# The first six row blocks of a weight, loaded in nine transfers instead of one, at the end of a decode kernel

## The chip, the cores and the metric

The kernel runs on one core of one Trainium2 chip. The metric is the device time of one execution in microseconds (us): the median of several runs.

## The reference, cut to what matters

One decode step mixes an attention block (a) and a small feed-forward block (b) by a gate that is computed from the input.

```python
x = A_x                                             # (2, 1, 512)
g = _sigmoid((x * gate_w).sum(-1, keepdims=True))
a = _A_ref(x, A_k_cache, A_v_cache, A_wq, A_wo)     # 2 x 32 heads, 4096 cached keys of 128, then @ wo
b = _B_ref(x, B_w1, B_w2)                           # relu(x @ w1) @ w2, inner size 1376
return g * a + (1 - g) * b
```

Keys and values are 64 MB each in bf16, wq and wo 4 MB each, w1 and w2 1.4 MB each. Nearly all that the kernel does in time is to bring 145 MB through the DMA engines.

## The kernel before, in words

All loads are issued by SyncE (SP) on one queue, in the order in which the program lists them, and the core's 16 DMA engines work that queue off. The order is w1, wq, ten key transfers, nine value transfers (`jobs` 0 to 8, each of 4 or 8 MB), wo in two pieces (`wo0` of 3 MB, `wo1` of 1 MB), and w2. Each transfer names a semaphore; each DMA engine that takes part adds 1 to it when its share has landed, and the reader waits for 16. Transfers that must not overwrite data still in use have a wait of SP ahead of them. w2 reuses the memory of the transposed keys and of the probabilities (the tile `kt`), so its first transfer waits until the last probabilities have been copied out (`pt_8_0` to `pt_8_3`). The later w2 transfers have no wait of their own.

The pieces of w2, of 128 partitions each, and their semaphores are, in order of issue (sizes for one partition):

- `w2a`: row block 10 (1 KB).
- `w2b`: row blocks 0 to 5 (6144 bytes, 768 KB in all). This is the transfer that is changed.
- `w2c`: row blocks 6 and 7 and the first half of 8 (2560 bytes).
- `w2d`, `w2e`, `w2f`: the first half of row block 9, the second half of 8, the second half of 9 (512 bytes, 64 KB in all, each).

In the sources these rows are contiguous: partition p holds rows 10p to 10p+9 of w2 (`w2_in`), 10 KB in a row, of which `w2b` takes the first 6 KB.

TensorE's order at the end is fixed by hand. It multiplies the last value unit (`v_unit(8)`, L461), gathers the heads (`o_gather`, L486 and L496), projects with wo (`project`, L508, which waits for `wo0` at its row 0 and `wo1` at its row 24), and then sums the feed-forward part into the bank `fin`: row block 10 (`ffn_f(10)`, waits for `w2a`), the projected attention (`wo_sum`, L540), row blocks 0 to 7 (`ffn_f(0)` to `ffn_f(7)`, L516, of which row block 0 waits for `w2b` and row block 6 for `w2c`), and row blocks 8 and 9 in `ffn_last` (L208), which waits for `w2d`, `w2e` and `w2f` in that order. VectorE and ScalarE copy the four quarters of the result out (L579, L581), and SP and ScalarE send one row of it each (L293).

The lines of the transfers are L282 (values), L283 and L284 (wo), L285 (`w2a`) and L290 (`w2b` to `w2f`). L600 is the end of the program, where each engine's list is written out.

## Time and profile before

| what | us |
|---|---|
| median of 3 runs | 344.19 (344.06 to 344.74) |
| profiled execution, first to last instruction (span) | 342.9 |
| median less span: what lies around the span | 1.3 |
| TensorE busy / VectorE busy in the span | 197.8 / 178.5 |
| DMA moved in the span | 145.46 MB read, mean 425 GB/s |
| share of the span in which the chain that ended last stood on DMA | 68% |

The profiled execution has no time of its own beside its span; the sums below are made on the span and set on the median, with the 1.3 us that lie around it taken as unchanged. Besides the page, the trace holds a record of each DMA packet (start, duration, size, queue) and of each semaphore increment; where the text speaks of one DMA engine, packets were joined to a chain, each at the end of the one before it, which works because the engines are never idle between 6 us and the end.

### The profile page before, as it was taken

The numbers are of one execution on the slowest core, as the hardware profiler recorded it, in microseconds if no ns is written. First come the engines' busy times: TensorE is split into PE (matmuls) and PEld (weight loads), VectorE is DVE, ScalarE is ACT, GpSimd is POOL, SyncE is SP. The second block draws the span as 40 slices with busy tenths as digits, with TensorE's granted clock in tenths as the row PEclk, the third lists the DMA queues.
The fourth block names the chain that finished last, engine by engine and source line by source line (L and its number), as shares of the span: only waits on it lengthen the run. The fifth ranks groups of instructions, "written<-read, shape, count | busy, mean of one in ns | idle before, by whom it ended". The sixth has DMA issues, their size and how long they took to land.

```text
span 342.9 us, 2540 instructions
## 1 busy us (share of the span) xinstructions
PE 197.8 (58%) x1228; PEld 54.3 (16%) x972; DVE 178.5 (52%) x127; ACT 23.1 (7%) x71; POOL 19.9 (6%) x36
## 2 busy tenths in 40 slices
PE   0177329799969799699799337220706043150656
PEld 0141001111111111111111013100303011020231
DVE  2239059899789899698999562220100103020121
ACT  1040000000000000000000240000000000000000
POOL 8000000000000000000000040110100101000000
PEclk9999959989999999989999858755656756565787
DMA  8998989899998999999999999999999999998996
GB/s 348 428 489 369 482 375 482 382 474 413 438 489 367 429 443 466 392 459 390 475 420 436 461 390 420 445 466 413 443 413 445 428 428 443 413 468 382 440 401 239
DMA packets 4196, 145.61 MB, mean 425 GB/s; under 512 B 469, under 2 KB 986, under 8 KB 1242
## 3 DMA queue, kind: packets, MB, share of 16 engines
q1 hardware_dynamic: 4178, 145.46, 98.5%
q8 instruction: 8, 0.13, 0.2%
q14 instruction: 2, 0.02, 0.0%
q10 hardware_dynamic: 8, 0.00, 0.0%
HBM read 145.46 MB, written 0.00 MB: 424 GB/s over the span
## 4 chain that ended last, share of the span: by engine, by line
DMA 68%; DVE 15%; PE 13%; ACT 1%; issue 1%; POOL 0%; SPq 0%; DVEq 0%
DMA kv<-in_A_k_cache_dram 31%; DMA kv<-in_A_v_cache_dram 23%; DVE kt L386 13%; DMA kt<-in_B_w_dram 9%; PE PS L461 6%; DMA kv<-in_A_wq_dram 4%; PE PS L407 3%; PE PS L197 3%; ACT kt L428 1%; PE PS L333 1%; DVE mpad L413 1%; DVE kt L471 1%; POOL ptm L444 0%; DVE qbuf L467 0%; DVE kt L432 0%
## 5 line engine op out<-in xcount | busy, mean ns | idle before, releaser
L386 DVE STREAM_TRANSPOSE kt<-kv 128x2048 f32<-128x2048 f32 x64 | 141.2, 2274 | 22.4 <-DMA kv<-in_A_k_cache_dram 22.3
L407 PE MATMUL PS<-kt,qbuf 128*128 128x512 bf16 x256 | 105.7, 413 | 31.8 <-DVE kt L386 26.3
L197 PE MATMUL PS<-kt,qbuf 128*128 128x512 bf16 x256 | 105.1, 411 | 0.0
L461 PE MATMUL PS<-kv,ptm 128*32 128x512 bf16 x512 | 46.5, 541 | 79.0 <-DMA kv<-in_A_v_cache_dram 76.0
L467 DVE TENSOR_TENSOR qbuf<-PS,maskc 128x512 f32<-128x512 f32 x9 | 6.2, 692 | 109.0 <-PE PS L461 109.0
L407 PEld LDWEIGHTS PS<-kt,qbuf 128*128 128x128 bf16 x256 | 25.5, 100 | 139.9 <-DVE kt L386 72.7
L461 PEld LDWEIGHTS PS<-kv,ptm 128*32 128x32 bf16 x512 | 19.0, 129 | 105.1 <-issue 98.6
L444 POOL COPY ptm<-kt 32x512 bf16<-32x512 bf16 (+1 forms) x18 | 11.5, 638 | 268.7 <-DVE rsum L475 175.6
L360 ACT ACTIVATE qbuf<-PS 32x8 bf16<-32x8 bf16 x40 | 7.9, 196 | 134.2 <-PE PS L197 132.7
L448 ACT ACTIVATE ptm<-kt 32x512 bf16<-32x512 bf16 (+1 forms) x9 | 5.3, 603 | 100.1 <-PE PS L461 98.7
L471 DVE TENSOR_REDUCE kt<-qbuf 128x128 f32<-128x512 f32 x9 | 9.3, 1028 | 0.3
L428 ACT ACTIVATE kt<-PS,negm 128x512 bf16<-128x512 f32 x8 | 5.4, 696 | 30.4 <-DVE negm L424 30.4
L333 PE MATMUL PS<-kv,xTw 128*32 128x512 bf16 x32 | 3.6, 629 | 5.9 <-DMA kv<-in_A_wq_dram 5.9
L478 PE MATMUL PS<-rsum,sell 128*32 128x1 f32 x4 | 0.4, 196 | 10.1 <-DVE rsum L475 10.1
L432 DVE STREAM_TRANSPOSE kt<-kt 128x1024 bf16<-128x1024 bf16 x4 | 5.0, 1245 | 1.7 <-ACT kt L428 1.4
L348 DVE CAST qrow<-PS 128x256 bf16<-128x256 f32 x2 | 2.4, 1396 | 6.4 <-PE PS L333 6.4
L508 PE MATMUL PS<-kv,oW 128*2 128x512 bf16 x32 | 3.4, 590 | 1.4 <-DMA kv<-in_A_wo_dram 1.4
L300 PE MATMUL PS<-ident,x_sb 3*128 3x3 bf16 x4 | 0.3, 166 | 6.2 <-DMA x_sb<-in_gate_w_dram 6.2
L486 PE MATMUL PS<-kt,selx 128*32 128x128 f32 x18 | 3.4, 328 | 0.3 <-DVE kt L471 0.3
L303 DVE COPY xT<-PS 128x12 bf16<-128x12 bf16 x1 | 0.2, 169 | 6.5 <-PE PS L300 6.5
L230 POOL MEMSET ptm<- 128x4096 bf16 x1 | 3.5, 3501 | 0.0
L413 DVE TENSOR_REDUCE mpad<-PS 128x1 f32<-128x2048 f32 x1 | 2.3, 2290 | 2.1 <-PE PS L197 2.1
(64 smaller groups left out, 44.2 us busy)
## 6 DMA issues: line engine op xcount, KB each, us to landing
kv<-in_A_k_cache_dram SPq DMA_DIRECT2D x4, 4096.0 KB, 31.6
kv<-in_A_v_cache_dram SPq DMA_DIRECT2D x2, 4096.0 KB, 27.0
kv<-in_A_wq_dram SPq DMA_DIRECT2D x1, 4096.0 KB, 15.0
kv<-in_A_wo_dram SPq DMA_DIRECT2D x1, 3072.0 KB, 29.3
kt<-in_B_w_dram SPq DMA_DIRECT2D x1, 1376.0 KB, 5.8
kv<-in_A_wo_dram SPq DMA_DIRECT2D x1, 1024.0 KB, 31.3
kt<-in_B_w_dram SPq DMA_DIRECT2D x1, 768.0 KB, 31.9
kt<-in_B_w_dram SPq DMA_DIRECT2D x1, 320.0 KB, 32.3
```

The source lines that it names most:

```text
L197: return e.add_instruction(mybir.InstMatmult(start_tensor_calc=start, stop_tensor_calc=stop, tile_size=(128, 128), tile_position=(0, 0), l ...
L333: pe(lambda e, n=n, t=t: e.matmul(psf(32 * (n % 4), 32 * (n % 4) + 32, (QR_B + n // 4) * BANK, 512), lhsT=xTw[:, t, :], rhs=wq_sb[:, t, n ...
L360: act(lambda a, hq=hq: a.activation(out=qbuf[32 * hq:32 * hq + 32, g % 2, :, :, 32 + 32 * hq], in_=cols[32 * hq:32 * hq + 32, u4 // 2, 2 * ...
L386: dve(lambda v: v.transpose(out=dst, in_=pairs[:, h, 64 * rr:64 * rr + 64]), waits=([f"pe_sc_{i - NKT}"] if i >= NKT else ["pe_h"] if i == ...
L407: return e.matmul(args[0], lhsT=args[1], rhs=args[2], start=first, stop=last)
L413: dve(lambda v: v.tensor_reduce(out=mpad[:, 0:1], in_=psf(0, 128, 0, 2048), axis=AX.X, op=ALU.max), waits=["pe_sc_63", "c_mpad"], signal=" ...
L428: act(lambda a, bk=bk, e2=e2: a.activation(out=blocks[:, bk, :, 16 * e2:16 * e2 + 16], in_=psf(0, 128, bk * BANK, 512).rearrange("p (r n) ...
L444: pool(lambda e, args=args: e.tensor_copy(**args), waits=waits, signal=f"pt_{j}_{hq}")
L448: act(lambda e, args=args: e.activation(func=ACT.Copy, **args), waits=waits, signal=f"pt_{j}_{hq}")
L461: pe(lambda e, m=m, t=t: e.matmul(psf(32 * t, 32 * t + 32, V_B[j % 2] * BANK, 512), lhsT=ptm[:, j % 2, 4 * m:4 * m + 4, :, :], rhs=rows[:, ...
L467: dve(lambda e: e.tensor_tensor(out=Y.rearrange("p (c d) -> p c d", c=4), in0=psf(0, 128, V_B[u % 2] * BANK, 512).rearrange("p (c d) -> p ...
L471: dve(lambda e: e.tensor_reduce(out=X2[:, u, :], in_=Y.rearrange("p (c d) -> p d c", c=4), axis=AX.X, op=ALU.add), waits=[f"dve_y{u}"], si ...
```

## The change

The rows of `w2b` are no longer fetched by one transfer of 128 partitions but by nine, which together cover the same partitions, with the same bytes for each. The first has 64 partitions (every second), the next 32 (every fourth from 1), the next 16 (every eighth from 3). The sixteen partitions left (7, 15, ..., 127) come in transfers of 5, 4, 3, 2, 1 and 1 rows. All nine add to the same semaphore, so TensorE now waits for 144 at row block 0 in place of 16. `w2a` stays ahead of them and `w2c` to `w2f` behind them in SP's list.

```diff
+    parts = [slice(0, 128, 2), slice(1, 128, 4), slice(3, 128, 8)]
+    parts += [slice(a, b + 1, 8) for a, b in ((7, 39), (47, 71), (79, 95), (103, 111), (119, 119), (127, 127))]
     for name, c0, c1 in (("w2b", 0, 3072), ("w2c", 3072, 4352), ("w2d", 4608, 4864), ("w2e", 4352, 4608), ("w2f", 4864, 5120)):
-        sp(lambda e, name=name, c0=c0, c1=c1: e.dma_start(w2f[:, c0:c1], w2_in[:, c0:c1]).then_inc(sem[name], 16))
+        for p in (parts if name == "w2b" else [slice(0, 128)]):
+            sp(lambda e, name=name, c0=c0, c1=c1, p=p: e.dma_start(w2f[p, c0:c1], w2_in[p, c0:c1]).then_inc(sem[name], 16))
...
-        dw = {10: [(sem["w2a"], 16)], 0: [(sem["w2b"], 16)], 6: [(sem["w2c"], 16)]}.get(r, [])
+        dw = {10: [(sem["w2a"], 16)], 0: [(sem["w2b"], 144)], 6: [(sem["w2c"], 16)]}.get(r, [])
```

## The prediction

> **What bounds the kernel now.** I read the chain that ended last first, then the stretches of the end, then SP's issues, then the single DMA packets.

> ```profile
> 305.92 1.02 DVE kt L471
> ...
> 308.17 32.26 DMA kt<-in_B_w_dram
> 340.43 0.04 issue
> 340.47 0.33 PE PS L516 x10
> 340.80 0.44 PE PS L208 x6
> 341.24 0.02 issue
> 341.27 0.28 DVE out_sb L579
> ```

> The chain of waits (start, duration): from 308.17 the end hangs on w2's transfers, which stand in the DMA queue behind values and wo. Compute comes in for the last 2.5 us only.

> ```profile
> 318.00:326.00 8.00, 5.37 (x64) 2.21 (x64) 1.71 (x2) 0.00 (x0) 0.00 (x0) 0.78 1.03 441
> ...
> 334.80:338.40 3.60, 3.40 (x36) 0.91 (x36) 0.00 (x0) 0.00 (x0) 0.00 (x0) 0.56 1.02 405
> 338.40:340.60 2.20, 1.17 (x50) 0.56 (x46) 0.69 (x1) 0.00 (x0) 0.00 (x0) 0.94 0.58 201
> ```

> Busy time by stretch; the last two columns are the DMA share and GB/s. The DMA engines are full until 338.4 and then run out one by one (share 0.58): they don't end together, and the last one sets the time.

> ```profile
> q8 instruction: 8, 0.13, 0.2%
> q14 instruction: 2, 0.02, 0.0%
> ```

> These ten packets (queue, packets, MB) are program code, and they explain the spread. Joined into chains, each of the ten lies on a different DMA engine. The eight engines that fetched 16 KB finish their last increment between 340.18 and 340.53; the two with 8 KB at 339.16 and 339.79; the six with none between 338.46 and 338.97. The mean of all 16 is 339.65, so levelling alone could bring 0.88 us at most.

> ```profile
> 339.65 0.51 PE L516 MATMUL PS<-kt,hT 128*2 128x128 bf16 x24
> 340.47 0.33 PE L516 MATMUL PS<-kt,hT 128*2 128x128 bf16 x10 [0.32 <-DMA kt<-in_B_w_dram]
> ...
> 340.66 0.57 PE L208 MATMUL PS<-kt,hT 128*2 128x128 bf16 x6
> ```

> TensorE's timeline follows the slowest engine: `w2b` has all 16 increments at 339.61, `w2c` at 340.43, `w2f` at 340.97. From there to the end (342.95) are 1.98 us that the change doesn't touch.

> ```profile
> 306.04 0.43 SPq L284 DMA_DIRECT2D kv<-in_A_wo_dram  x1
> 307.33 0.33 SPq L285 DMA_DIRECT2D kt<-in_B_w_dram  x1
> 307.70 10.74 SPq L290 DMA_DIRECT2D kt<-in_B_w_dram  x5
> ```

> SP's issues: one takes 0.43 us, but five take 10.74. Single records show four of 0.43 and the fifth, `w2f`, of 8.84 us: it stood until 318.44. It has no wait in the code. Nine transfers were then on their way (value jobs 7 and 8, `wo0`, `wo1`, `w2a` to `w2e`), and job 7 landed on its last engine at 317.83, 0.18 us before a normal issue that ends at 318.44 would begin. Before, this costs nothing: `w2f` is needed 20 us later.

> **The change part by part.**

> Bytes per engine. `x` with two rows left one packet and one increment on each of two engines, `gate_w` with one row on one engine. So I take n rows below 16 to go over n engines, one each, and 64, 32 and 16 over all 16. Every engine then has 4+2+1 = 7 rows where it had 8, and the engine that the one-row transfers use has one more from each of six: 13. I could find that one: the packet of `gate_w` at 5.24 lies in the chain that ends at 338.51, without a code fetch. A `w2b` row took 0.239 us on the slowest engine (337.226 to 339.138 for eight). For an engine that loses one: -0.239. The nearest row for an increment packet is 6 ns to the next packet, and there are two more: +0.012. Sum **-0.23 us** for the late engines. The fullest engine: 338.51 + 5 x 0.239 + 8 x 0.006 = 339.75, under the 340.30 of the late ones. [...]

> Which engines serve the transfers of 5, 4, 3 and 2 rows, no row shows beyond the first. If a late one (340.53) has two rows more instead of one less, it ends 0.48 later; if none has, no cost. I take none, as the one engine known is early.

> Cost per transfer. Row: `w2d`, `w2e` and `w2f` are 64 KB each and land 0.17 us apart (340.62, 340.79, 340.97), back to back with no gap on any engine. So small transfers in a full queue cost bytes and 6 ns. [...]

> SP's issues. Eight more at 0.43 are 3.5 us, hidden by the 20 us that SP runs ahead; if that cover is gone, each counts. And it goes, if a tenth transfer on its way must always wait for the oldest. Issued freely would be the parts of 64, 32, 16 and 5 rows (the ninth). The 4-row part waits for job 7 (318.4), the 3-row part for job 8 (landed 327.54), the first 2-row part for `wo0` (334.86 + 0.18 + 0.43 = 335.47), the next for `wo1` (337.36, so 337.97), the last for `w2a` (337.72; SP is free at 337.97, so 338.40). Then `w2c` waits for the 64-row part: latest engine 337.226 + 4 x 0.239 = 338.18, increment seen 0.45 later (340.52 to 340.97 for `w2f`), so 338.63 + 0.18 + 0.43 = 339.24. `w2d` waits for the 32-row part: 339.12, issued 339.73. `w2e` (16 rows) follows SP's own pace, 340.16, `w2f` 340.59. From an issue's end to its first packet 0.47 us (result row: 341.93 to 342.40): 341.06; its eight 512-byte packets and increment 0.19; seen 0.45 later: 341.70 in place of 340.97, **+0.74 us**. Queued behind SP's waiting issue are just these transfers; TensorE waits for them, then the copies. Bounds of this term: if the limit counts something else (descriptors, or each engine by itself, where the early engines free places early) it is 0; if any transfer that has landed frees a place, the small parts have done so by 338.4, `w2c` to `w2f` follow at SP's pace to 340.13, and `w2f` is seen at 341.25: +0.28. I take +0.74, since the one release that is seen came 0.18 after the oldest transfer had landed on its slowest engine.

> TensorE's wait for 144 instead of 16 is the same instruction. The saved 0.23 is swallowed then, since `w2f`'s arrival is set by SP.

> **Forecast.** 344.19 + 0.74 = **344.93 us**, slower. It needs both that the limit counts transfers and that it frees in order: chance 0.38.

> **Rivals.**

> *Levelled as planned* (the other side): the limit doesn't bind, engines are bound by their own pace, late ones have a row less. 344.19 - 0.23 = 343.96. For it: a descriptor runs at 24576 bytes in 0.913 us or 26.9 GB/s whichever engine has it. It decides if the places in the queue are freed by each engine for itself; then the first engine, which holds all parts, is the tightest, has done its 64-row share at 336.2, and `w2f` is out by 339.1, before the late engines want it at 340.1. Chance 0.20.

> *Engines that share a way into SBUF.* In every 128-partition transfer each engine has eight partitions, and nothing shows two engines writing into one group. With spaced rows they might: eight partitions reached by one way of 26.9 GB/s, two engines in it at half pace. Bounds: none share, 0; all seven common rows at half pace, +7 x 0.239 = +1.67, less the row, +1.45. Between: the late engines start `w2b` spread over 0.34 us (336.89 to 337.23), two of them on average 0.11 apart. In the first part (two rows into one group, then two into another) each loses 0.96 - 0.22 = 0.74, in the second 0.48 - 0.22 = 0.26, in the third 0.24 - 0.11 = 0.13: 1.13 less 0.23 = +0.90, so 345.09. Also, the sixteen odd rows would still go into the late engines' groups, whoever carries them. Against it: nothing in this trace was ever slowed so. [...] Chance 0.36.

> *A late engine among the first five.* 0.48 worked out above: 344.67. Chance 0.06.

> **Numbers.** About 0.2% (0.69 us) is what a measurement of this kernel can tell from no change. Of the forecast's 0.38, 0.28 is slower and 0.10 same (its 0.28 bound); of the shared ways' 0.36, 0.28 and 0.08; of the levelling's 0.20, 0.16 same and 0.04 faster, should more have been uneven than the profiled run shows; of the last, 0.03 and 0.03. Faster 0.04, same 0.37, slower 0.59. The two slow mechanisms can add up: 0.74 + 0.90 = 1.64, 345.83. The range reaches from just under the levelled case, 343.90, to 345.80. The slow cases' own range is 344.45 to 345.80.

> **What would show it.** Forecast: several issues of L293 and its neighbours stand for us until 338 or later, a gap in the late engines' packets ahead of `w2c` to `w2f`, and `w2f`'s last increment near 341.7. Levelled: SP free by 339, last increment near 340.74, the early engines ending near 339.7. Shared ways: 6144-byte packets near 480 ns in place of 239, no gaps. Wrong altogether: if the last value or wo increments move, or if the end after `w2f` is not 1.98 us.

## The result, and the profile after

| | before | after |
|---|---|---|
| median, us | 344.25 (344.04 to 344.80, 15 runs) | 344.87 (344.68 to 345.38, 15 runs) |
| span of the profiled execution, us | 342.9 | 343.4 |
| last increments of `w2a`, `w2b`, `w2f`, us | 337.72, 339.61, 340.97 | 337.59, 340.04, 341.38 |
| mean of `w2f`'s 16 landings, us; last less mean | 340.17; 0.80 | 340.80; 0.58 |
| mean of a 6144-byte packet, ns | 241.6 | 298.6 |

The ratio is 1.002, with an interval of 1.0013 to 1.0027: slower by 0.62 us (0.45 to 0.93). The forecast was 344.93. The number came out, but by luck: the reason that the forecast gave isn't what happened, as the views show one after the other.

The end of the chain of waits of after (start, duration, engine, line):

```profile
309.21 0.83 SPq L293
310.09 0.64 SPq L293
310.77 0.71 SPq L293
311.52 0.59 SPq L293
312.15 0.42 SPq L293
312.91 27.84 DMA kt<-in_B_w_dram
340.79 0.33 PE PS L519 x10
341.12 0.54 PE PS L208 x6
341.68 0.28 DVE out_sb L582
```

The last link to the end is still DMA; the chain of before stood on it from 308.17 to 340.43. SP's issues of the parts now show up ahead of it, all nine done by 312.9. They only lead into a transfer that then lies in the queue for 28 us.

SP's issues of after:

```profile
306.97 0.33 SPq L285 DMA_DIRECT2D kt<-in_B_w_dram  x1
307.34 22.73 SPq L293 DMA_DIRECT2D kt<-in_B_w_dram  x13
342.03 0.27 SPq L296 DMA_DIRECT2D out_dram<-out_sb  x1
```

Thirteen issues in 22.73 us, done at 330.07. The single records: the nine parts take 0.26 to 0.83 each, `w2c` and `w2d` go out without a stop as well, `w2e` stands for 3.37, `w2f` for 12.88 us. The forecast had SP standing until 340.6. Here the last issue ends some 9 us before its first packet starts (about 339.4), with up to 16 transfers on their way. So SP isn't late.

TensorE's timeline of after:

```profile
339.00 0.40 PE L543 MATMUL PS<-qbuf,selw 128*2 128x128 f32 x8 [0.68 <-DVE qbuf L514]
340.08 0.51 PE L519 MATMUL PS<-kt,hT 128*2 128x128 bf16 x24 [0.69 <-DMA kt<-in_B_w_dram]
340.79 0.33 PE L519 MATMUL PS<-kt,hT 128*2 128x128 bf16 x10 [0.20 <-DMA kt<-in_B_w_dram]
341.01 0.64 PE L208 MATMUL PS<-kt,hT 128*2 128x128 bf16 x6
```

Row block 0 starts 0.43 later than before (339.65), after the longest wait for a transfer; the last piece, `w2f`, lands 1.34 us after `w2b`, before 1.36. From `w2f`'s last landing to the end are 343.4 - 341.38 = 2.0 us, as before (1.98). The time is therefore lost while `w2b` is fetched. Busy time by stretch of after (last two columns: DMA share, GB/s):

```profile
318.00:326.00 8.00, 5.02 (x64) 2.16 (x56) 1.71 (x2) 0.00 (x0) 0.00 (x0) 0.80 1.00 430
334.80:338.40 3.60, 3.52 (x36) 0.84 (x30) 0.15 (x1) 0.00 (x0) 0.00 (x0) 0.53 1.02 354
338.40:340.60 2.20, 0.91 (x32) 0.43 (x32) 0.54 (x1) 0.00 (x0) 0.00 (x0) 1.00 0.80 226
```

The engines are just as busy from 334.8 to 338.4 (share 1.02) but move 354 GB/s in place of 405. They are not waiting for work; each packet takes longer. By start time, the 6144-byte packets take 240 to 248 ns until 336.5, 266 then, and from 337.0 on 368, 335, 332, 344 (means of half microseconds, as the rates that follow); the total rate falls from 413 GB/s to 294, 281 and 294. The stretch comes on all 16 engines within 0.3 us, also on those that are still in the first part of 64 rows. It comes shortly after the early engines have got to the part of 16 (about 336.6).

The code fetches, the cause of the uneven ends, are as before:

```profile
q8 instruction: 8, 0.13, 0.2%
q14 instruction: 2, 0.02, 0.0%
```

### The profile page after: what moved, and what is told of

It is laid out like the page before. It is cut to its first block, busy times and chain, and to the rows that moved or that the text cites. A ratio compares the mean times of both kernels' runs of the same rounds, so it can differ in the third digit from the quotient of the medians.

```text
span 343.4 us, 2548 instructions
## 1 busy us (share of the span) xinstructions
PE 197.6 (58%) x1228; PEld 54.5 (16%) x972; DVE 178.5 (52%) x127; ACT 23.1 (7%) x71; POOL 19.9 (6%) x36
## 4 chain that ended last, share of the span: by engine, by line
DMA 66%; DVE 15%; PE 13%; SPq 2%; ACT 1%; issue 1%; POOL 0%; DVEq 0%
DMA kv<-in_A_k_cache_dram 31%; DMA kv<-in_A_v_cache_dram 23%; DVE kt L389 13%; DMA kt<-in_B_w_dram 8%; PE PS L464 6%; DMA kv<-in_A_wq_dram 4%; PE PS L410 3%; PE PS L197 3%; SPq L293 2%; ACT kt L431 1%; PE PS L336 1%; DVE mpad L416 1%; DVE kt L474 1%; POOL ptm L447 0%; DVE qbuf L470 0%
```

## The experiments

"Stretch" below is one number for each kernel: the sum, over all packets of w2 from 330 us on, of the duration less the mean for that size in e9 (the least of all: 46.1, 240.5, 103.4 and 27.0 ns for 1024, 6144, 2560 and 512 bytes), divided by 16 engines. A "one-row share" is what an engine gets from a transfer of at most 16 rows: one row of 6144 bytes, then an increment (after has 517 packets under 512 bytes, before 469; the 48 more are one increment for each engine of each added transfer: 16, 16, 5, 4, 3, 2, 1 and 1). In e2, e5 and e6 the packets have other sizes; their times stand with the runs. In every run row block 0 waits for 16 increments of each transfer that `w2b` has.

| kernel | parts of `w2b` | median, us | ratio to before (95%) | stretch, us | one-row shares |
|---|---|---|---|---|---|
| before | 128 | 344.25 | | 0.01 | 0 |
| after | 64, 32, 16, 5, 4, 3, 2, 1, 1 | 344.87 | 1.0013 to 1.0027 | 0.82 | 32 |
| e1 | 64 even, 64 odd | 344.14 | 0.9989 to 1.0007 | 0.01 | 0 |
| e4 | as after, source rows in a row | 344.76 | 1.0007 to 1.0024 | 0.76 | 32 |
| e3 | 0 to 63, 64 to 127 | 347.06 | 1.0071 to 1.0096 | 2.05 | 0 |
| e7 | 64, 32, 16 | 344.54 | 0.9997 to 1.0014 | 0.35 | 16 |
| e8 | 64, 32, 16, 16 | 344.90 | 1.0012 to 1.0030 | 0.64 | 32 |
| e9 | 64, 32, 32 | 344.34 | 0.9990 to 1.0008 | 0 | 0 |
| e10 | 64, 16 from 1, 3, 5, 7 | 345.77 | 1.0029 to 1.0054 | 1.42 | 64 |
| e11 | 64, 16 from 1, 5, 3, 7 | 345.46 | 1.0021 to 1.0044 | 0.92 | 64 |
| e12 | 64, 32, five of 6, 2 | 345.67 | 1.0022 to 1.0050 | 0.74 | 32 |

The kernels before, in the three groups of runs that were compared, had 344.25 (e1 to e4), 344.22 (e5 to e8) and 344.37 (e9 to e12).

**e1: two transfers of every second row.**

```diff
-    parts = [slice(0, 128, 2), slice(1, 128, 4), slice(3, 128, 8)]
-    parts += [slice(a, b + 1, 8) for a, b in ...]
+    parts = [slice(0, 128, 2), slice(1, 128, 2)]
```

> w2b in two transfers of 64 spaced partitions (the even ones, then the odd ones); every engine has eight rows, as before. Shared ways: all eight rows of 6144 bytes are written beside another engine's into the same group of partitions, so the packets take 300 to 330 ns in place of 239 throughout, the late engines need 8 x 0.32 = 2.56 us in place of 1.91, and the time is about 344.25 + 0.65 = 344.9. Queue limit, number of small transfers, or uneven rows as the cause: one transfer more and nothing uneven, so 344.25 and packets of 239 ns.

344.14, the same as before, and 6144-byte packets of 241 ns. Busy time by stretch of e1:

```profile
334.80:338.40 3.60, 3.45 (x36) 0.87 (x36) 0.04 (x1) 0.00 (x0) 0.00 (x0) 0.57 1.01 400
338.40:340.60 2.20, 1.20 (x47) 0.62 (x46) 0.65 (x1) 0.00 (x0) 0.00 (x0) 0.93 0.51 176
```

400 GB/s: rows 2 apart cost nothing. The shared-ways rival, as worked out in the prediction, had its largest loss (0.74 us) in the first part of 64 rows, which e1 has too; that working has fallen.

**e2: nine transfers of all 128 partitions, each a ninth of the columns.**

```diff
+    cuts = [336 * i for i in range(9)] + [3072]
-        sp(lambda e, ...: e.dma_start(w2f[p, c0:c1], w2_in[p, c0:c1]).then_inc(sem["w2b"], 16))
+        # for each pair of cuts a, b: w2f[:, a:b] from w2_in[:, a:b]
```

> w2b in nine transfers again, but each of all 128 partitions and a ninth of the columns (672 bytes a row, the last 768). Shared ways: no engine writes into another's group, so only the shorter rows cost: 72 packets of some 30 ns in place of 8 of 239, about +0.2, so 344.3 to 344.5. Number of transfers or queue limit as the cause: as slow as the change or slower, 344.9 and more, since all nine go to all 16 engines.

344.71 (1.0004 to 1.0022). SP's issues of e2:

```profile
306.61 0.33 SPq L285 DMA_DIRECT2D kt<-in_B_w_dram  x1
306.99 27.59 SPq L292 DMA_DIRECT2D kt<-in_B_w_dram  x9
334.62 1.86 SPq L294 DMA_DIRECT2D kt<-in_B_w_dram  x4
```

With nine full pieces SP does stand (27.59 us for nine issues), and is out at 336.5, still ahead of the need. The loss has another place: a 672-byte packet takes 35.4 ns, and with the 3 ns by which packets overlap (before, eight of 241.6 ns take 1.91 us) a row in nine pieces takes, as an estimate, 9 x 32.4 = 292 ns where it took 237; 8 rows of each engine make 0.44, of 0.46 measured. Nine increments for each engine cost nothing that is left to see. The time is above what was expected without a price for transfers (344.5 at most), by this cost of the short rows. So neither the number of transfers nor SP makes the time of after.

**e3: the lower and the upper half.**

```diff
+    parts = [slice(0, 64), slice(64, 128)]
```

> w2b in two transfers of 64 neighbouring partitions (0 to 63, then 64 to 127); eight rows for each engine. Shared ways: an engine shares its group with another one of the 16, but if the groups of the upper half belong to the late engines, the two that share are 1.5 us out of step and share part of the time: between the packets of before and those of the change, +0.25 (0 to +0.6), so 344.5. All others: 344.25.

347.06, and busy time by stretch:

```profile
334.80:338.40 3.60, 3.08 (x32) 0.78 (x32) 0.00 (x0) 0.00 (x0) 0.00 (x0) 0.62 1.03 292
338.40:340.60 2.20, 0.88 (x20) 0.20 (x12) 0.69 (x1) 0.00 (x0) 0.00 (x0) 1.00 1.01 214
```

214 GB/s with all engines busy (1.01), and 6144-byte packets of 395 ns in the mean, 559 at most. So the place of the rows can halve the rate: 214 is about half of the 405 GB/s at which before runs from 334.8 to 338.4, with the engines as busy (1.02), and e1, with as many rows in each of its two transfers, has 400. Why it does so no run shows.

**e4: the same destinations, but source rows that lie one after the other.**

```diff
+    at = [0, 64, 96, 112, 117, 121, 124, 126, 127, 128]
-            ... e.dma_start(w2f[p, c0:c1], w2_in[p, c0:c1])
+            ... e.dma_start(w2f[p, c0:c1], w2_in[at[i]:at[i + 1], c0:c1])
```

> The nine transfers write the same spaced partitions as the change, but each reads neighbouring rows of w2 (so rows land in other partitions: the order of the rows of row blocks 0 to 5 is left out of the computation). Shared ways into SBUF: nothing changes, 344.87, packets of about 320 ns. Reading spaced rows as the cause: packets back to 239 ns and 344.0 to 344.3.

344.76, packets of 296 ns, stretched as after's. The order in which the source is read isn't the cause.

**e5 and e6: short rows by eight engines.** One transfer of 128 partitions takes 5376 of the 6144 bytes, and sixteen transfers of eight partitions take the other 768; e6 leaves eight of these out (those of partitions 64 to 127).

```diff
+    pieces = [(slice(0, 128), 0, 2688)]
+    pieces += [(slice(b + j, b + j + 29, 4), 2688, 3072) for b in (0, 32, 64, 96) for j in range(4)]   # e6: b in (0, 32)
```

> w2b as one transfer of 128 partitions with seven eighths of the columns, and the last eighth (768 bytes a row) in sixteen transfers of 8 partitions (every fourth), so that eight engines carry it for all 16: the late ones have an eighth less, as in the change, without its 64-, 32- and 16-row parts. If the eight are the early ones and engines are bound by their own pace: -0.23, 344.0. Shared ways: the rows of the upper half are written beside the late engines' own rows into their groups, which eats most or all of that: 344.1 to 344.5. Number of small transfers as the cause: seventeen in place of nine, slower than the change, 345 and more.

> As the run before it, but the eight small transfers into partitions 64 to 127 are left out, and with them a part of w2 in row block 5. [...] Number of small transfers as the cause: still slower than before.

347.06 (1.0067 to 1.0094) and 345.42 (1.0020 to 1.0045). Here a transfer does have a price. Most 768-byte packets take 36 ns and follow each other at once, but the increments of the slowest engines land 0.2 us apart (e5, the last: 342.00, 342.19, 342.39, 342.59; e6: 339.90, 340.10, 340.29, 340.49). The engines run ahead of their increments and stand later: in e5 sixteen packets of 2560 bytes, behind the short rows, take 505 to 620 ns, and in e6 single 512-byte packets up to 199. All other packets of 2560 bytes take 102 to 135 ns in e5 and 102 to 114 in e6. So it is not the stretch of after, which is on all engines. In e6 only two of the eight engines that carry the short rows are late ones (they begin their 5376-byte rows at 336.67, four others at 335.2 to 335.3), which supports the prediction's choice that the first five are early ones.

**e7 and e8: which parts cost.** e7 leaves the last 16 rows out; e8 fetches them as one part of 16.

```diff
+    parts = [slice(0, 128, 2), slice(1, 128, 4), slice(3, 128, 8)]                       # e7
+    parts = [slice(0, 128, 2), slice(1, 128, 4), slice(3, 128, 8), slice(7, 128, 8)]     # e8
```

> The change with its first three parts (64, 32 and 16 partitions) alone; the last sixteen rows of row blocks 0 to 5 are left out. If the transfers of 5 to 1 rows, written by the first engines into other engines' groups, are what stretches the packets: back to 239 ns, and the late engines have seven rows: 344.0. If the 32- or 16-row part puts two engines into one group: still stretched from about 336.5 on, 344.3 to 344.7.

> The whole of w2b in parts of 64, 32, 16 and 16 spaced partitions: eight rows for every engine, nothing below 16 rows. Small parts as the cause: 344.2, packets of 239 ns. The 16-row parts as the cause (two engines in one group, half of the groups unused): both of them are stretched, 2 x 0.24 more at most on the late engines and more if it spreads to their neighbours, 344.5 to 344.9.

Busy time by stretch of e7 and of e8, where before has 405 GB/s:

```profile
334.80:338.40 3.60, 3.52 (x36) 0.83 (x35) 0.13 (x1) 0.00 (x0) 0.00 (x0) 0.53 1.01 370
334.80:338.40 3.60, 2.12 (x36) 0.70 (x36) 0.49 (x1) 0.00 (x0) 0.00 (x0) 1.00 1.02 364
```

e7: 344.54, not told from before by its interval although every engine has a row less; e8: 344.90, with eight rows on every engine and no part under 16. So neither the uneven rows nor the very small parts are needed for the loss: a second part of 16 alone makes it as large as after's. In e7, too, all engines slow down together, from 337.0 on (302, 279, 268 ns).

**e9 to e12: 32 rows or 16, and another way to level.**

```diff
+    parts = [slice(0, 128, 2), slice(1, 128, 4), slice(3, 128, 4)]                                    # e9
+    parts = [slice(0, 128, 2)] + [slice(i, 128, 8) for i in (1, 3, 5, 7)]                             # e10
+    parts = [slice(0, 128, 2)] + [slice(i, 128, 8) for i in (1, 5, 3, 7)]                             # e11
+    parts = [slice(0, 128, 2), slice(1, 128, 4), slice(3, 24, 4), slice(27, 48, 4), slice(51, 72, 4),
+             slice(75, 96, 4), slice(99, 120, 4), slice(123, 128, 4)]                                 # e12
```

> Parts of 64 (every second row), 32 (1, 5, 9, ...) and 32 (3, 7, 11, ...) in place of the nine; no rows moved between engines. [...] Theory 'mixing' (any part of fewer than 64 rows makes two engines write into one group, whatever the step): the two parts carry as many rows as the two 16-row parts of the four even parts and more (32 each), so at least that kernel's +0.65: 344.9 or more, packets up to 340 ns.

> 64 rows, then the odd rows as four parts of 16 rows 8 apart, from 1, 3, 5 and 7 in this order. [...] Mixing: four 16-row parts, each at about half of the 0.65 that two of them cost: +1.3, 345.5 us.

> [...] Mixing: the order makes no difference: 345.5 us, as the order 1, 3, 5, 7.

> 64 rows (every second), 32 rows (1, 5, 9, ...), and the last 32 rows (3, 7, 11, ...) as five transfers of 6 neighbouring ones of them and one of 2, which the first six engines carry. So the late engines lose two rows (-0.48), the first six get three or four more (+0.72 to +0.96 on ends of 338.5 to 339.2, so 339.9 or less if the sixth isn't a late one). [...] Mixing: stretched as the nine parts, 344.6 us or more. If the sixth engine is a late one it ends 0.7 later than before: 345 us, without a stretch.

Busy time by stretch, 334.8 to 338.4 and on, of e9:

```profile
334.80:338.40 3.60, 3.26 (x36) 0.92 (x36) 0.00 (x0) 0.00 (x0) 0.00 (x0) 0.60 1.02 405
338.40:340.60 2.20, 1.20 (x43) 0.44 (x36) 0.69 (x1) 0.00 (x0) 0.00 (x0) 0.88 0.59 209
```

of e10:

```profile
334.80:338.40 3.60, 2.18 (x36) 0.70 (x36) 0.15 (x1) 0.00 (x0) 0.00 (x0) 1.00 1.02 328
338.40:340.60 2.20, 0.52 (x12) 0.11 (x8) 0.55 (x1) 0.00 (x0) 0.00 (x0) 0.99 0.92 217
```

and of e12:

```profile
334.80:338.40 3.60, 2.97 (x32) 0.96 (x36) 0.01 (x1) 0.00 (x0) 0.00 (x0) 0.53 1.03 385
338.40:340.60 2.20, 0.72 (x20) 0.13 (x12) 0.69 (x1) 0.00 (x0) 0.00 (x0) 1.00 0.85 236
```

e9 keeps 405 GB/s and the time of before: "mixing" has fallen. e10 and e11 lose about what "mixing" had said for four parts of 16 (1.40 and 1.09 us, where it had 1.3), but the order counts by 0.31 us, which "mixing" had not said. e12 was to level the ends further and is slower than before by 1.30: the rows of its small transfers are 4 apart, as those of e9's parts of 32, which cost nothing, and its packets are stretched all the same (290.6 ns in the mean, 379 in the half microsecond from 338.0). So the step from row to row alone doesn't decide it. Not all of the 1.30 is w2b's: in the profiled execution of e12 `w2a` had landed 0.44 us later than in e9 (338.30, 337.86), with packets that were not stretched, and why isn't known.

What orders all of these runs is the last column of the table. Kernels in which no engine ever has a single row of `w2b` as its share of a transfer have no stretch (before, e1, e9); the others have 0.32 to 0.41 engine-microseconds for each one-row share (stretch x 16, over the shares: e7 0.35, e8 0.32, after 0.41, e4 0.38, e12 0.37, e10 0.36), with e11 below at 0.23. Such a row, 0.24 us long, goes with some 0.35 us more, and all 16 engines pay it together. This order was read from the runs once all were done; no further run was made to test it. e3, which has no such share and the longest stretch, is another matter.

## Why the prediction was right, and where it was not

**The row that the late engines lose (-0.23): held.** `w2f` lands last 0.80 us after the mean of the 16 engines before, 0.58 after: -0.22. e4, with the same parts, has 0.58 too; of the kernels with eight rows on every engine, e8 has 0.73 and e9 0.89, so the gain is known to some 0.1 only. The mean itself moved by +0.63, and the profiled execution of after ran 0.13 us ahead at `w2a`, so by some 0.76; the stretch is 0.82. Levelling gain and stretch make 0.82 - 0.22 = +0.60, and +0.62 was measured.

**The late engine among the first five: not seen.** Had one carried two rows more, the last landing would have moved away from the mean, not towards it.

**SP's issues (+0.74): the step that failed.** "A tenth transfer on its way must always wait for the oldest" was read from one standing issue, and the same record allowed the other readings that stood as its lower bound. Sixteen were on their way in after, and the cost of the term was 0, that bound. The limit isn't a number of transfers, as the last four issues of e8, then of e10, show:

```profile
309.31 8.98 SPq L293 DMA_DIRECT2D kt<-in_B_w_dram  x4
310.01 2.00 SPq L293 DMA_DIRECT2D kt<-in_B_w_dram  x4
```

In e8 `w2f` stood for 7.41 us with twelve transfers on their way; in e10 it went out in 0.43 with thirteen. What SP's limit counts is open: in e2 as many transfers as in after, all of 128 partitions, made it stand from the fifth piece on (9.4, 7.9, 5.7 and 2.1 us).

**Bytes and 6 ns for each transfer: the term that was mis-sized.** It came from transfers of which each engine has eight packets, and was applied to shares of one. For those, 0.35 engine-microseconds each, 32 of them over 16 engines, should have stood there: about +0.7. Eight more transfers had no fixed cost of microseconds each: the whole change is 0.62.

**Shared ways (345.09): nearest in what it shows, wrong in its working.** No gaps and longer 6144-byte packets: as that rival said. That eight partitions are reached by one way no run shows. And the packets mostly took 320 to 370 ns, not 480; not pairs but all engines slowed; and the parts of 64 and 32 rows, which made 1.00 of its 1.13 us, cost nothing (e1, e9).

**Levelled as planned (343.96):** its gain came, and the slower pace cost almost four times as much (0.82 against 0.22).

So the forecast's time was met by luck: a term of +0.74 that wasn't there stood in for one of +0.82 - 0.22 that was.

**What stays open** is why one-row shares slow every engine. Two readings are left. One: a share of a single row with its increment is dear in itself. Against it stands that in e7 the own single rows of five of the six earliest engines took 236 to 242 ns, while the rows of the others were stretched, and that e5 and e6 have 128 and 64 shares of one row of 768 bytes, but no such stretch: apart from e5's sixteen, no packet of 2560 bytes took over 135 and 114 ns there (after: 202 at most, 137 in the mean). The other, a guess: a transfer of 16 or fewer rows is dealt to the engines so that they write where others are busy, and writes that can't be taken hold up all. For it speak e3, where the place of the rows halves the rate (214 for 405 GB/s), and the order in e10 and e11 (0.31 us). The records name no engine and no address, so no run shows where an engine writes, or tells the two readings apart.

## What to carry to other kernels

When engines end unevenly, compare the mean of their ends as well as the last one: a re-cut transfer can close the gap (here by 0.22 us) and slow the mean by more (0.63). When a transfer of such rows must be cut, try first a cut in which every engine keeps two or more rows of each part, by spaced rather than by neighbouring partitions: 64 + 64 and 64 + 32 + 32 spaced rows cost nothing here, parts of 16 some 0.35 us each, neighbouring halves 2.8. And a queue that stands once shows a limit, not what it counts: take the bound at which the wait is harmless as seriously as the other.
